# A chunk-attention and MLP kernel: half of tile 1's first product in seven products, its scores and side work moved

## The chip, the cores and the metric

The kernel runs on one core of a Trainium2 chip. The metric is the device time of one execution in microseconds. TensorE multiplies matrices into PSUM banks; VectorE, ScalarE and GpSimd (DVE, ACT and POOL in the profile) read and write them or on-chip memory; SyncE (SP) issues the DMAs. Each engine takes its instructions in order, and waits are made from the data dependencies of the program.

## The reference

Attention within chunks of 64 positions, then an MLP with exact Gelu:

```python
q_c = q.reshape(B, H, nc, 64, D)             # B = 8, H = 8, S = 576, D = 64, nc = 9
scores = scale * (q_c @ k_c.T);  attn = softmax(scores);  out = attn @ v_c
x = out.transpose(0, 2, 1, 3).reshape(B * S, H * D)      # 4608 x 512
y = gelu(x @ w_in) @ w_out                               # 512 -> 2048 -> 512
```

## The kernel before

The 4608 tokens are cut into nine tiles of 512: tile t below 8 has the first 512 positions of batch t, and tile 8 has the last chunk of each batch. Tiles are counted from 0. Work is in bf16 with float32 sums in PSUM. Each tile has two stages: `mm1` computes h = gelu(x w_in) as 16 slices of 128 hidden features, and `mm2` computes y = h w_out. The attention of tile t + 1 is put by hand between the matmuls of tile t; `phase(t, e1, e2)` gives what is put where, keyed by slot or by word.

**A plain slice** of `mm1` is four matmuls of 512 columns into one bank and a gelu on ScalarE (L470 for tiles 0 and 1, L595 in later ones).

**mm1 in groups** (L559, tiles 2 to 8) does half of the slices, in two groups a and b of four slices each, by Strassen's scheme in Winograd's form: seven products (`prod`, L572) of four matmuls of 256 columns each stand for the eight that four plain slices amount to. They use sums of blocks of w_in (made once, in tile 0) and of x (`x_sums`, L548: four subtractions on VectorE). The seven land in three banks X, Y, Z per group; between them copies and additions run. `PROGRAM` (L556) is the order, and its words are: `1a` is product 1 of group a; `c1a` copies X to a new Y on ScalarE; `c2a` copies Y out on ScalarE and `c3a` on VectorE (L616); `a1a` and `a2a` add Z to these copies on VectorE (L619); `g22a` is the gelu of a block (L590); `p` is a plain slice; `h1` to `h3` form sums of h, in tiles from 3 on. Product 3 accumulates in Y and waits until c3 has read it; product 4 accumulates in Z and waits until a1 has read it. The plain slices use the two banks of the pool `ps_tp`, products X and Z the three of `ps_at`, Y and the slots of mm2 the three of `ps_mm`.

**mm2** of tiles 1 and 2 has 16 slots of four matmuls of 512 columns; slot s computes quarter s % 4 of the sum for token block s // 4. From tile 3 on (`FIRST7`), mm2 too is done in seven products (L645), each of 16 matmuls of 256 columns, out of sums of w_out (`w_sums`) and of h.

**Attention of tile n** (called in mm2 of tile n - 1): `quad_S` (L223) computes the scores by 64 small matmuls into two banks of `ps_tp` and two of `ps_at`, and ScalarE takes four exps, after `act_table(Exp)` has loaded its table; `quad_parts` (L240) sums them by transposes and reductions on VectorE; `quad_total` goes on to the reciprocals; `quad_av` multiplies by v and `quad_x` writes the tile's x on VectorE. `x_sums` follows. In `one_tile` (L960), used for tiles 2 and 3, these stand at slots 0, 3 and 7 of mm2. From tile 3's mm2 on, `quad_av` stands behind the first of mm2's products and the scores of the tile after next behind the fourth.

**The k reorder.** k of tile 3 arrives transposed in another order of columns (`k_u`), and `in_order` (L195) copies it in four pieces on VectorE; the scores of tile 3 read the result.

Of the kernel before, what the change touches and what calls it, by code (L numbers as in the profile page):

```python
# [11 lines left out]
def kernel(  # L12
# [9 lines left out]
    nc = tc.nc  # L22
    P = 128
    f32 = mybir.dt.float32
    bf16 = mybir.dt.bfloat16
# [5 lines left out]
    J = 4  # L31
# [160 lines left out]
            st[nm + "t"] = flips.tile([P, G * J, P], bf16, tag=nm + "t", name=f"{nm}_t")  # L192
        nc.sync.dma_start_transpose(st[nm + "t"][:], st[nm][:].rearrange("p g j r d -> p (g j r d)"))  # L193

    def in_order(t):  # L195

        st = tiles[t]
        raw, st["kt"] = st["kt"], flips.tile([P, G * J, P], bf16, tag="kt", name="k_t")
        for g in range(G):
            DV(st["kt"][:, g * J:(g + 1) * J].rearrange("p n (e j) -> p (n e) j", j=J),  # L200
               raw[:, g * J:(g + 1) * J].rearrange("p j e -> p e j"))

# [264 lines left out]
        return T  # L467


    def mm1_slot(t, f, n=1, between={}):  # L470
        st = tiles[t]
        if f == 0:
            st["h"] = hpool.tile([P, FF, MT], bf16, tag="h", name="h")
        banks = [(ps_mm, "mm")] + [(ps_at, "at") if t == 1 else (ps_mm, "mm")] * (n - 1)
        h_ps = [pool.tile([P, MT], f32, tag=tag, name="h_ps") for pool, tag in banks]
        for ks in range(KS):
            for u in between.get(ks, ()):
                u()
            for a in range(n):
                o = f_of(t, f + a)  # L480
                nc.tensor.matmul(h_ps[a][:], w_in_sb[:, ks, o * P:(o + 1) * P], st["x"][:, ks, :],  # L481
                                 start=(ks == 0), stop=(ks == KS - 1))
        for a in range(n):
            nc.scalar.activation(st["h"][:, f_of(t, f + a), :], h_ps[a][:], Act.Gelu)  # L484

    def mm1_begin(t, n):

# [12 lines left out]
    def f_of(t, f):  # L500
        return f if t < FIRST7 else f // 2 + FH * (f % 2)

    def h_blocks(t, j0, j1):
        st = tiles[t]
# [40 lines left out]
        x = tiles[t]["x"][:].rearrange("p (c k) (n m) -> p c k n m", c=2, n=2)  # L545
        return x[:, 0, :, 0], x[:, 0, :, 1], x[:, 1, :, 0], x[:, 1, :, 1]

    def x_sums(t):  # L548

        b11, b12, b21, b22 = x_blocks(t)  # L550
        own = work.tile([P, 4, 2, TH], bf16, tag="x_t", name="x_t", bufs=1)
        T = tiles[t]["T"] = [None] + [own[:, i] for i in range(4)]
        for i, a, b in ((1, b12, b11), (3, b22, b12), (2, b22, T[1]), (4, b21, T[2])):
            nc.vector.tensor_tensor(T[i], a, b, op=mybir.AluOpType.subtract)
# [4 lines left out]
    def mm1_groups(t, extra):  # L559
# [5 lines left out]
        T, w = st["T"], in_blocks()  # L565
        TT, add = nc.vector.tensor_tensor, mybir.AluOpType.add
        banks, sums = {}, {}
        tags = {"a": ("y_1", "y_2"), "b": ("y_5", "y_2")}
        plain = [j + FH * r for j in (2, 3, 6, 7) for r in range(2)]
        hs = {"h1": (0, 4), "h2": (4, 7), "h3": (7, 8)}  # L570

        def prod(g, n):  # L572
            q = "ab".index(g)
            lhs, rhs, name, fresh = {
                1: (w[:, 0, :, 0, q], b11, "X", True), 2: (w[:, 1, :, 0, q], b21, "X", False),
                3: (w_s[4][:, :, q], b22, "Y", False), 4: (w[:, 1, :, 1, q], T[4], "Z", False),
                5: (w_s[1][:, :, q], T[1], "Y", False), 6: (w_s[2][:, :, q], T[2], "Y", False),
                7: (w_s[3][:, :, q], T[3], "Z", True)}[n]
            if fresh:
                banks[g + name] = ps_at.tile([P, 2, TH], f32, tag="at", name=f"h_{name}")  # L580
            for i in range(2):
                for kk in range(2):
                    nc.tensor.matmul(banks[g + name][:, i], lhs[:, kk, i], rhs[:, kk], start=fresh and i == kk == 0,  # L583
                                     stop=(kk == 1), skip_group_check=True)

        def gelu(g, r, m):
            j = 4 * "ab".index(g) + FH * r
            src = {(0, 0): lambda: banks[g + "X"], (0, 1): lambda: banks[g + "Y"],
                   (1, 0): lambda: sums[g, 0], (1, 1): lambda: sums[g, 1]}[r, m]()
            nc.scalar.activation(h[:, j:j + 2, m], src[:], Act.Gelu)  # L590

        for word in PROGRAM.split():
            for u in extra.get(word, ()):
                u()
            if word == "p":  # L595
                f = plain.pop(0)
                bank = ps_tp.tile([P, MT], f32, tag="tp", name="h_ps")
                for ks in range(KS):
                    nc.tensor.matmul(bank[:], w_in_sb[:, ks, f * P:(f + 1) * P], st["x"][:, ks, :],  # L599
                                     start=(ks == 0), stop=(ks == KS - 1))  # L600
                nc.scalar.activation(st["h"][:, f, :], bank[:], Act.Gelu)  # L601
            elif word in hs:
                if t >= FIRST7:
                    h_sums(t, *hs[word])
            elif word[0].isdigit():
                prod(word[1], int(word[0]))
            elif word[0] == "g":
                gelu(word[3], int(word[1]) - 1, int(word[2]) - 1)
            elif word[:2] == "c1":
                g = word[2]  # L610
                banks[g + "Y"] = ps_mm.tile([P, 2, TH], f32, tag="mm", name="h_Y")
                AC(banks[g + "Y"][:], banks[g + "X"][:])
            elif word[:2] in ("c2", "c3"):
                g, i = word[2], int(word[1]) - 2
                sums[g, i] = work.tile([P, 2, TH], f32, tag=tags[g][i], name=tags[g][i], bufs=1)
                (AC if i == 0 else DV)(sums[g, i][:], banks[g + "Y"][:])  # L616
            elif word[0] == "a":
                g, i = word[2], 2 - int(word[1])
                TT(sums[g, i][:], banks[g + "Z"][:], sums[g, i][:], op=add)  # L619
# [142 lines left out]
    def phase(t, extra1, extra2, by_rows=False, between={}, begun=0):  # L762
        nms = MT // P
        order = [(ms, qt) for ms in range(nms) for qt in range(NQ)]
        if by_rows:
            order = [(None, f) for f in range(FF - FC)] + [(ms, NQ - 1) for ms in range(nms)]
        first = begun or (3 if t == 1 else 1)
        if t >= FIRST71:
            mm1_groups(t, extra1)
        elif not begun:  # L770
            mm1_slot(t, 0, first, between)
        for f in range(first, FF if t < FIRST71 else 0):
            for u in extra1.get(f, ()):
                u()
            mm1_slot(t, f)
            if t >= FIRST7 and f in (7, 13, 15):
                h_sums(t, *{7: (0, 4), 13: (4, 7), 15: (7, 8)}[f])
# [61 lines left out]
    with tc.manual_schedule():  # L839
# [131 lines left out]

        pool_cast_qk(2)
        for t in range(1, NT):
# [4 lines left out]
            if t == 1:  # L978
# [3 lines left out]
                loads_of_qk(3)  # L982
                pool_cast_qk(3)
                load_v_rows(3)
                e1 = {3: [lambda: w_sums((1, 3))]}
                e2 = one_tile(2, {5: [lambda: act_table(Act.Gelu)],
                                  8: [lambda: flips_of(3), lambda: loads_of_qk(4)]})
            elif t == 2:
                cast_v_rows(3, PO)
                pool_cast_qk(4)  # L990
                e1 = {"3b": [lambda: in_order(3)], "h2": [lambda: w_sums((2, 4))]}
                flips_of(4)
                loads_at(2)
                cast_v_rows(4, PO)
# [2 lines left out]
            elif n < NT:  # L997
# [9 lines left out]
                else:  # L1007
# [44 lines left out]
```

## Time and profile before

| what | value |
|---|---|
| median of 3 runs | 278.72 us (278.70 to 278.88) |
| the profiled execution | 278.58 us |
| its span, first to last instruction | 276.8 us |
| mean granted TensorE clock | 0.997 |
| TensorE busy | 262.3 us, 95% |
| VectorE busy | 196.3 us, 71% |
| ScalarE busy | 172.9 us, 62% |

A line of the timeline has its start and length in microseconds, the engine, the source line, the operation, what it writes and reads, the tile's partitions and columns, and the count; in brackets stands the idle time of the engine before it and what ended it. Successive lines of TensorE overlap by its pipeline: the distance of two starts is what the stream costs, the length also holds the passage through the array.

### The profile page before, as it was taken

Reading aid. Unit: us, or ns where it says so; the run is one execution under the profiler, and the core shown is the slowest. Engines: PE = TensorE matmul, PEld = TensorE weight load, DVE = VectorE, ACT = ScalarE, POOL = GpSimd, SP = SyncE. Lnnn points to the kernel's source line nnn. Section 1 sums busy time; section 2 is a strip of 40 time slices with the busy share of each in tenths; the row PEclk is TensorE's granted clock in tenths of the full one; section 3 lists DMA queues with packets and bytes.
Section 4 is the critical chain, followed back from the end, with each engine's and each line's share of the span. In section 5 each row is a group of like instructions: output and inputs, shape, how many; then the busy total and the mean of one; then the engine's idle time right before and its main releaser. Section 6 shows DMA issues by size and latency. Waiting matters only on the chain.

```text
span 276.8 us, 7097 instructions
## 1 busy us (share of the span) xinstructions
PE 262.3 (95%) x2864; PEld 175.8 (64%) x2889; DVE 196.3 (71%) x348; ACT 172.9 (62%) x333; POOL 92.9 (34%) x180
## 2 busy tenths in 40 slices
PE   7789999999999699999999999999999999999993
PEld 3454454444456344668876887688768876886682
DVE  3664677901973999879967995899589958943842
ACT  2567746778638664886758666766675777328600
POOL 3635665541710823450372262108511311000000
PEclk9999999999999999999999999999999999999998
DMA  6999999998999977997999949896853310130005
GB/s 209 278 370 401 395 381 253 250 254 245 253 220 262 230 167 165 268 255 180 288 268 200 267 129 219 200 181 174 156 133 85 112 38 2 37 108 9 2 0 152
DMA packets 118064, 53.93 MB, mean 195 GB/s; under 512 B 93456, under 2 KB 112912, under 8 KB 118032
## 3 DMA queue, kind: packets, MB, share of 16 engines
q1 hardware_dynamic: 117712, 52.97, 73.0%
q8 instruction: 22, 0.36, 0.5%
q10 hardware_dynamic: 320, 0.52, 0.5%
q14 instruction: 10, 0.08, 0.1%
HBM read 36.70 MB, written 9.44 MB: 167 GB/s over the span
## 4 chain that ended last, share of the span: by engine, by line
PE 56%; DMA 14%; SPq 13%; DVE 7%; issue 3%; POOL 3%; ACT 2%; POOLq 0%; DVEq 0%; ACTq 0%
PE y_ps L637 23%; PE h_ps L599 14%; PE h_Y L583 6%; PE y_ps L735 5%; SPq L126 5%; DMA arrival<-in_q_dram 5%; DMA arrival<-in_v_dram 4%; PE h_X L583 4%; PE h_Z L583 4%; DMA arrival<-in_k_dram 3%; DMA arrival<-in_moe_w_in_dram 3%; SPq L193 2%; SPq L106 2%; SPq L112 2%; SPq L145 2%
## 5 line engine op out<-in xcount | busy, mean ns | idle before, releaser
L599 PE MATMUL h_ps<-x,w_in_sb 128*128 128x512 bf16 x211 | 54.7, 379 | 0.7
L601 ACT ACTIVATE h<-h_ps 128x512 bf16<-128x512 f32 x56 | 33.3, 595 | 14.8 <-PE h_ps L599 14.5
L637 PEld LDWEIGHTS <-h_s 128*128 128x128 bf16 x384 | 37.2, 98 | 4.6
L160 POOL CAST q_nat<-arrival 128x512 bf16<-128x512 f32 x33 | 22.2, 712 | 48.4 <-DMA arrival<-in_q_dram 33.3
L637 PE MATMUL y_ps<-w_t,h_s 128*128 128x256 bf16 x288 | 34.2, 273 | 0.2
L735 PE MATMUL y_ps<-w_out_sb,h 128*128 128x512 bf16 x138 | 31.3, 379 | 0.8 <-issue 0.8
L599 PEld LDWEIGHTS <-w_in_sb 128*128 128x128 bf16 x224 | 21.9, 98 | 16.0
L637 PEld LDWEIGHTS <-h 128*128 128x128 bf16 x288 | 28.2, 98 | 5.0 <-issue 0.5
L160 POOL CAST k_nat<-arrival 128x512 bf16<-128x512 f32 x34 | 23.3, 722 | 15.0 <-DMA arrival<-in_k_dram 9.3
L619 DVE TENSOR_TENSOR y<-h_Z,y 128x512 f32<-128x512 f32 x28 | 19.3, 690 | 10.9 <-PE h_Z L583 10.5
L583 PEld LDWEIGHTS <-w_in_s 128*128 128x128 bf16 x224 | 21.9, 98 | 8.0 <-issue 1.8
L481 PE MATMUL h_ps<-x,w_in_sb 128*128 128x512 bf16 x114 | 25.4, 379 | 0.5 <-DVE x L367 0.4
L207 POOL CAST v_nat<-arrival 128x1024 bf16<-128x1024 f32 x14 | 15.6, 1128 | 26.3 <-DMA arrival<-in_v_dram 26.3
L616 DVE COPY y<-h_Y 128x512 f32<-128x512 f32 x14 | 9.7, 691 | 19.9 <-PE h_Y L583 19.9
L735 PEld LDWEIGHTS <-h 128*128 128x128 bf16 x144 | 13.4, 98 | 15.6 <-issue 0.2
L637 PE MATMUL y_ps<-w_out_sb,h 128*128 128x256 bf16 x192 | 22.9, 273 | 0.0
L484 ACT ACTIVATE h<-h_ps 128x512 bf16<-128x512 f32 x29 | 17.0, 598 | 7.7 <-PE h_ps L481 7.6
L251 DVE STREAM_TRANSPOSE pt<-pT 128x256 f32<-128x256 f32 x28 | 12.2, 435 | 12.8 <-ACT pT L236 12.8
L837 ACT ACT_TABLE_LOAD x16 | 20.5, 1283 | 1.0 <-PEq L1036 0.7
L590 ACT ACTIVATE h<-y 128x512 bf16<-128x512 f32 x28 | 17.6, 627 | 5.7 <-DVE y L619 5.3
L583 PEld LDWEIGHTS <-w_in_sb 128*128 128x128 bf16 x168 | 16.4, 98 | 6.8
L481 PEld LDWEIGHTS <-w_in_sb 128*128 128x128 bf16 x116 | 11.3, 98 | 14.2 <-issue 0.7
(125 smaller groups left out, 446.4 us busy)
## 6 DMA issues: line engine op xcount, KB each, us to landing
out_dram<-y_sb SPq DMA_DIRECT2D x32, 256.0 KB, 2.9
arrival<-in_q_dram SPq DMA_DIRECT2D x7, 1024.0 KB, 6.3
arrival<-in_k_dram SPq DMA_DIRECT2D x24, 256.0 KB, 6.0
arrival<-in_v_dram SPq DMA_DIRECT2D x42, 128.0 KB, 3.1
arrival<-in_moe_w_out_dram SPq DMA_DIRECT2D x4, 1024.0 KB, 11.3
arrival<-in_v_dram SPq DMA_DIRECT2D x8, 256.0 KB, 5.8
arrival<-in_moe_w_in_dram SPq DMA_DIRECT2D x4, 512.0 KB, 7.6
arrival<-in_moe_w_in_dram SPq DMA_DIRECT2D x2, 1024.0 KB, 9.8
```

Source lines behind the costliest of these rows:

```text
L160: copy(st[nm][:, g].rearrange("p j r d -> p r j d"), st[nm + "f"][:, 2 * g:2 * g + 2])
L207: copy(st["v"][:, r::2], st["vf"][:, r::2])
L481: nc.tensor.matmul(h_ps[a][:], w_in_sb[:, ks, o * P:(o + 1) * P], st["x"][:, ks, :], start=(ks == 0), stop=(ks == KS - 1))
L484: nc.scalar.activation(st["h"][:, f_of(t, f + a), :], h_ps[a][:], Act.Gelu)
L583: nc.tensor.matmul(banks[g + name][:, i], lhs[:, kk, i], rhs[:, kk], start=fresh and i == kk == 0, stop=(kk == 1), skip_group_check=True)
L590: nc.scalar.activation(h[:, j:j + 2, m], src[:], Act.Gelu)
L599: nc.tensor.matmul(bank[:], w_in_sb[:, ks, f * P:(f + 1) * P], st["x"][:, ks, :], start=(ks == 0), stop=(ks == KS - 1))
L601: nc.scalar.activation(st["h"][:, f, :], bank[:], Act.Gelu)
L619: TT(sums[g, i][:], banks[g + "Z"][:], sums[g, i][:], op=add)
L637: nc.tensor.matmul(out[m], lhs[:, f, m * P:(m + 1) * P], rhs[:, f, :], start=fresh and f == 0 and (m == 0 or len(out) == 3), stop=(f == FH ...
L735: nc.tensor.matmul(y_ps[:], st["h"][:, f, ms * P:(ms + 1) * P], w_out_sb[:, f, :], start=(f == 0), stop=(f == FF - 1))
L837: nc.scalar.activation(act_scratch[:], rest[:, 0:1], func)
```

## The change

- Tile 1's mm1 is done in groups too (`FIRST71` 1 instead of 2), by an order of its own, `LATE`. It begins with three plain slices worked together (`start`, as tile 1 did before) and then forms the sums of x of tile 1 (`sums`). It has no `p` between 7b and 2b or between 3b and 4b, and no `p` after 4b. The banks of `p` are those of `ps_tp`.
- `w_sums((1, 3))` moves from behind tile 1's first three slices to the end of its mm1.
- `quad_S` and `quad_parts` of tiles 2 and 3 move from slot 0 to slot 1 of mm2; `act_table(Exp)` stays at slot 0.
- The four copies of `in_order(3)`, all at the word `3b` of tile 2, are done two at `3b` and two at `g21b`, so that `a2b` stands between them.
- In mm2 of tiles 3 to 7, `x_sums` is done as (1, 3) and (2, 4), with the addition at L678 and its store between the two.

```diff
-    def in_order(t):
+    def in_order(t, g0):
         st = tiles[t]
-        raw, st["kt"] = st["kt"], flips.tile([P, G * J, P], bf16, tag="kt", name="k_t")
-        for g in range(G):
+        if g0 == 0:
+            st["k_u"], st["kt"] = st["kt"], flips.tile([P, G * J, P], bf16, tag="kt", name="k_t")
+        raw = st["k_u"]
+        for g in (g0, g0 + 1):
...
-    FIRST7, FIRST71 = 3, 2
+    FIRST7, FIRST71 = 3, 1
...
-    def x_sums(t):
+    def x_sums(t, which=(1, 3, 2, 4)):
...
+        of = {1: (b12, b11), 3: (b22, b12), 2: (b22, T[1]), 4: (b21, T[2])}
+        for i in which:
+            a, b = of[i]
             nc.vector.tensor_tensor(T[i], a, b, op=mybir.AluOpType.subtract)

     PROGRAM = """begin 1a c1a 7a p 2a 6a c2a g11a 1b c1b p 5a c3a a1a 7b p 2b g22a 6b c2b 3a g11b g12a 4a a2a
                  p g21a 5b c3b a1b totals rc0 p 3b g22b g12b p 4b h1 a2b p g21b h2 p h3"""
+    LATE = """begin start sums p 1a c1a 7a p 2a 6a c2a g11a 1b c1b p 5a c3a a1a 7b 2b g22a 6b c2b 3a g11b g12a 4a a2a
+              p g21a 5b c3b a1b p 3b g22b g12b 4b a2b g21b end"""
...
-        for word in PROGRAM.split():
+        for word in (LATE if t == 1 else PROGRAM).split():
             for u in extra.get(word, ()):
                 u()
+            if word == "start":
+                mm1_slot(t, [plain.pop(0) for _ in range(3)], between)
+            elif word == "sums":
+                x_sums(t)
...
-            at = {0: [lambda: act_table(Act.Exp), lambda: quad_S(n), lambda: quad_parts(n)],
+            at = {0: [lambda: act_table(Act.Exp)], 1: [lambda: quad_S(n), lambda: quad_parts(n)],
...
-                e1 = {3: [lambda: w_sums((1, 3))]}
+                e1 = {"end": [lambda: w_sums((1, 3))]}
...
-                e1 = {"3b": [lambda: in_order(3)], "h2": [lambda: w_sums((2, 4))]}
+                e1 = {"3b": [lambda: in_order(3, 0)], "g21b": [lambda: in_order(3, 2)], "h2": [lambda: w_sums((2, 4))]}
...
-                      2: [lambda: x_sums(n)]}
+                      2: [lambda: x_sums(n, (1, 3))], 3: [lambda: x_sums(n, (2, 4))]}
...
-                    e2[3] = [lambda: quad_part(n + 1, 0, 0), lambda: quad_part(n + 1, 0, 1)]
+                    e2[3] += [lambda: quad_part(n + 1, 0, 0), lambda: quad_part(n + 1, 0, 1)]
```

More of the change, by code (lines that the diff above doesn't have):

```diff
@@ L467, in att_units, with mm1_slot @@
         return T
-    def mm1_slot(t, f, n=1, between={}):
+    def mm1_slot(t, fs, between={}):
         st = tiles[t]
-        if f == 0:
+        if "h" not in st:
             st["h"] = hpool.tile([P, FF, MT], bf16, tag="h", name="h")
-        banks = [(ps_mm, "mm")] + [(ps_at, "at") if t == 1 else (ps_mm, "mm")] * (n - 1)
+        banks = [(ps_mm, "mm")] + [(ps_at, "at")] * (len(fs) - 1)
         h_ps = [pool.tile([P, MT], f32, tag=tag, name="h_ps") for pool, tag in banks]
@@ L478, in mm1_slot @@
                 u()
-            for a in range(n):
-                o = f_of(t, f + a)
-                nc.tensor.matmul(h_ps[a][:], w_in_sb[:, ks, o * P:(o + 1) * P], st["x"][:, ks, :],
+            for a, f in enumerate(fs):
+                nc.tensor.matmul(h_ps[a][:], w_in_sb[:, ks, f * P:(f + 1) * P], st["x"][:, ks, :],
                                  start=(ks == 0), stop=(ks == KS - 1))
-        for a in range(n):
-            nc.scalar.activation(st["h"][:, f_of(t, f + a), :], h_ps[a][:], Act.Gelu)
+        for a, f in enumerate(fs):
+            nc.scalar.activation(st["h"][:, f, :], h_ps[a][:], Act.Gelu)
     def mm1_begin(t, n):
@@ L546, in x_blocks @@
         return x[:, 0, :, 0], x[:, 0, :, 1], x[:, 1, :, 0], x[:, 1, :, 1]
-    def x_sums(t):
+    def x_sums(t, which=(1, 3, 2, 4)):
         b11, b12, b21, b22 = x_blocks(t)
-        own = work.tile([P, 4, 2, TH], bf16, tag="x_t", name="x_t", bufs=1)
-        T = tiles[t]["T"] = [None] + [own[:, i] for i in range(4)]
-        for i, a, b in ((1, b12, b11), (3, b22, b12), (2, b22, T[1]), (4, b21, T[2])):
+        if "T" not in tiles[t]:
+            own = work.tile([P, 4, 2, TH], bf16, tag="x_t", name="x_t", bufs=1)
+            tiles[t]["T"] = [None] + [own[:, i] for i in range(4)]
+        T = tiles[t]["T"]
+        of = {1: (b12, b11), 3: (b22, b12), 2: (b22, T[1]), 4: (b21, T[2])}
+        for i in which:
+            a, b = of[i]
             nc.vector.tensor_tensor(T[i], a, b, op=mybir.AluOpType.subtract)
@@ L557, with mm1_groups @@
                  p g21a 5b c3b a1b totals rc0 p 3b g22b g12b p 4b h1 a2b p g21b h2 p h3"""
-    def mm1_groups(t, extra):
+    LATE = """begin start sums p 1a c1a 7a p 2a 6a c2a g11a 1b c1b p 5a c3a a1a 7b 2b g22a 6b c2b 3a g11b g12a 4a a2a
+              p g21a 5b c3b a1b p 3b g22b g12b 4b a2b g21b end"""
+    def mm1_groups(t, extra, between={}):
         st = tiles[t]
@@ L564, in mm1_groups @@
         b11, b12, b21, b22 = x_blocks(t)
-        T, w = st["T"], in_blocks()
+        w = in_blocks()
         TT, add = nc.vector.tensor_tensor, mybir.AluOpType.add
@@ L573, in prod @@
             q = "ab".index(g)
[L574 to L578, printed above, removed]
+            if n in (1, 2):
+                lhs, rhs, name = w[:, n - 1, :, 0, q], b11 if n == 1 else b21, "X"
+            elif n == 3:
+                lhs, rhs, name = w_s[4][:, :, q], b22, "Y"
+            elif n == 4:
+                lhs, rhs, name = w[:, 1, :, 1, q], st["T"][4], "Z"
+            else:
+                lhs, rhs, name = w_s[n - 4][:, :, q], st["T"][n - 4], "Z" if n == 7 else "Y"
+            fresh = n in (1, 7)
             if fresh:
@@ L590, in gelu @@
             nc.scalar.activation(h[:, j:j + 2, m], src[:], Act.Gelu)
-        for word in PROGRAM.split():
+        for word in (LATE if t == 1 else PROGRAM).split():
             for u in extra.get(word, ()):
                 u()
-            if word == "p":
+            if word == "start":
+                mm1_slot(t, [plain.pop(0) for _ in range(3)], between)
+            elif word == "sums":
+                x_sums(t)
+            elif word == "p":
                 f = plain.pop(0)
@@ L766, in phase @@
             order = [(None, f) for f in range(FF - FC)] + [(ms, NQ - 1) for ms in range(nms)]
-        first = begun or (3 if t == 1 else 1)
         if t >= FIRST71:
[L769 to L777, printed above, removed]
+            mm1_groups(t, extra1, between)
+        else:
+            for f in range(begun, FF):
+                mm1_slot(t, [f])
         if t >= FIRST7:
```

2 lines of the change are left out of this document (removed).

## The prediction

> **What bounds the kernel now.** Tiles are counted from 0. I read the page first, then the engines' busy time by stage, then TensorE's list of waits, and last the merged timeline around each place that the diff touches.
>
> ```profile
> PE 262.3 (95%) x2864; PEld 175.8 (64%) x2889; DVE 196.3 (71%) x348; ACT 172.9 (62%) x333; POOL 92.9 (34%) x180
> ```
> ```profile
> 50.67:65.10 14.43, 14.01 (x64) 6.16 (x63) 4.64 (x7) 10.17 (x18) 5.47 (x8) 1.00 1.00 233
> 65.10:80.37 15.27, 15.06 (x192) 7.45 (x193) 11.94 (x24) 9.72 (x24) 7.66 (x11) 1.00 0.89 262
> 80.37:93.61 13.24, 13.13 (x87) 8.49 (x87) 7.28 (x11) 9.75 (x18) 3.17 (x4) 1.00 1.04 238
> 93.61:111.86 18.25, 15.72 (x254) 8.04 (x257) 16.79 (x28) 10.69 (x27) 6.84 (x7) 1.00 0.81 188
> ```
> ```profile
> PE s_ps L229 <- ACT h L601: 2.1, 1, 2.1
> PE y_ps L637 <- DVE y_sb L678: 0.3, 1, 0.3
> ```
>
> The second fence has mm1 of tile 1, mm2 of tile 1, mm1 of tile 2 and mm2 of tile 2, with length and busy time of PE, PEld, DVE, ACT and POOL. TensorE fills three of the four; mm2 of tile 2 is 18.25 us long with 15.72 busy. The third fence gives the reason: one wait of 2.1 us before tile 3's scores. So the time is the sum of what TensorE streams plus a few waits, and in mm2 of tile 2 VectorE (16.79 of 18.25) is nearly as full as TensorE. That last fact limits the gain below.
>
> **Part 1: mm1 of tile 1 in groups.**
>
> ```profile
> 52.50 12.68 PE L481 MATMUL h_ps<-x,w_in_sb 128*128 128x512 bf16 x57 [0.37 <-DVE x L367]
> 52.96 2.34 DVE L631 TENSOR_TENSOR w_t<-w_out_sb 128x2048 bf16<-128x2048 bf16 x2
> 65.21 0.60 ACT L484 ACTIVATE h<-h_ps 128x512 bf16<-128x512 f32 x1 [0.27 <-PE h_ps L481]
> 67.23 2.04 ACT L236 ACTIVATE pT<-s_ps 128x512 bf16<-128x512 f32 x4
> 67.84 0.45 DVE L251 STREAM_TRANSPOSE pt<-pT 128x256 f32<-128x256 f32 x1 [12.54 <-ACT pT L236]
> 78.68 1.24 DVE L554 TENSOR_TENSOR x_t<-x 128x512 bf16<-128x512 bf16 x2
> 80.81 0.60 PE L583 MATMUL h_Z<-x_t,w_in_s 128*128 128x256 bf16 x4
> 82.11 0.60 PE L583 MATMUL h_X<-x,w_in_sb 128*128 128x256 bf16 x4
> 82.54 0.60 PE L583 MATMUL h_Y<-x_t,w_in_s 128*128 128x256 bf16 x4
> ```
>
> One record of the 58 matmuls from 52.50 to 65.10 is missing: 12.60/58 is close to 0.216 us for a matmul of 512 columns, 0.864 for a plain slice of four. A product of four matmuls of 256 columns takes 82.54 - 82.11 = 0.43 to 0.44 (0.109 each). The change removes 8 plain slices (6.91 us) and adds 14 products (6.11): TensorE saves 0.80.
>
> By the sustained spacing in the Trainium skill's page "TensorE: Matmul & The Clock Gate", section "Back-to-back issue gap" (131 ns at 512 columns, 81 at 128, so an estimate of 98 at 256 on a straight line), 32 matmuls of 4.2 us would become 56 of 5.5 us, 1.3 us lost instead of 0.8 won. The trace disagrees with both figures here: 216 and 109 ns.
>
> Waits come back. The first twelve matmuls are as before and end at 52.50 + 6 x 0.216 = 53.80. The new sums of x (two at 1.24 together, two shorter) start on VectorE where w_sums stood, at 52.96, so the one that the second product needs is there at 54.2; a plain slice and the first product lie ahead of it, to 55.1. They cost nothing, by 0.9 us of cover. At the end, tile 2's rows show what the new order does:
>
> ```profile
> 89.06 1.03 PE L599 MATMUL h_ps<-x,w_in_sb 128*128 128x512 bf16 x4
> 89.32 0.69 DVE L616 COPY y<-h_Y 128x512 f32<-128x512 f32 x1 [0.66 <-PE h_Y L583]
> 90.04 0.69 DVE L619 TENSOR_TENSOR y<-h_Z,y 128x512 f32<-128x512 f32 x1
> 90.06 0.60 PE L583 MATMUL h_Y<-x,w_in_s 128*128 128x256 bf16 x4
> ```
>
> There the plain slice ends at 89.93 and product 3b starts at 90.06, when c3b has read its bank: 0.13 lost. LATE has the same slice there, but none between 3b and 4b. 3b would end at 90.50 and 4b cannot write before a1b has read the bank, at 90.73: 0.25 to 0.30 lost. With 0.05 for small hand-offs earlier, the rest of mm1 takes 5 x 0.864 + 14 x 0.436 + 0.13 + 0.28 + 0.05 = 10.9 and ends at 64.7 instead of 65.10: 0.40 won, half of the 0.80.
>
> ScalarE ends later. It has 20 operations from 53.6 on (8 plain gelus, 8 of products, 4 copies); at 0.60 each that is 65.6. The last gelu waits for a2b: 4b ends at 64.7, VectorE starts 0.25 later (as c3b in the rows above), 0.69, then a gelu of 0.63: 66.3. Now the last gelu ends at 65.81 and the exps start 1.42 later, behind the table load. So the exps of tile 2 move from 67.23 to 67.7, 0.5 later. Putting the scores one slot later costs nothing: they are then done by 66.5 (64.7, 0.86 for the slot, twice 0.45 for such scores in part 2's rows), ahead of the table. w_sums (1, 3), moved behind a2b, runs from 65.6 to 68.0 on a VectorE that waits for the first exp until 68.3 (67.84 and 0.5): hidden, by 0.3 us. From the exps VectorE works without a gap to the sums of x, so the one that tile 2's second product needs slips from 79.92 to 80.4, while TensorE would want it at 80.81 - 0.40 = 80.4. The slack of 0.9 is used up exactly. I take 0.05 of wait: **0.35 won** at tile 2's second product.
>
> **Part 2: end of tile 2's mm1, scores of tile 3.**
>
> ```profile
> 90.65 3.67 DVE L200 COPY k_t<-k_u 128x512 bf16<-128x512 bf16 x4
> 91.36 0.60 PE L583 MATMUL h_Z<-x_t,w_in_sb 128*128 128x256 bf16 x4
> 93.61 0.45 PE L229 MATMUL s_ps<-q_t,k_t 64*64 64x64 bf16 x32
> 94.24 0.68 DVE L619 TENSOR_TENSOR y<-h_Z,y 128x512 f32<-128x512 f32 x1
> 94.84 2.96 DVE L631 TENSOR_TENSOR w_t<-w_out_sb,w_t 128x2048 bf16<-128x2048 bf16 x2
> 94.95 0.63 ACT L590 ACTIVATE h<-y 128x512 bf16<-128x512 f32 x1 [1.50 <-DVE y L619]
> 95.49 0.58 ACT L601 ACTIVATE h<-h_ps 128x512 bf16<-128x512 f32 x1
> 96.12 0.45 PE L229 MATMUL s_ps<-q_t,k_t 64*64 64x64 bf16 x32 [2.06 <-ACT h L601]
> 96.72 5.99 PE L735 MATMUL y_ps<-w_out_sb,h 128*128 128x512 bf16 x27 [0.16 <-issue]
> 98.10 0.45 DVE L251 STREAM_TRANSPOSE pt<-pT 128x256 f32<-128x256 f32 x1 [0.30 <-ACT pT L236]
> ```
>
> The 2.06 us is a queue of three. The scores' second half needs the bank of the last plain slice; its gelu stands on ScalarE behind g21b; g21b needs a2b; a2b stands on VectorE behind all four copies of the k reorder, 3.67 us, though its product 4b was done near 92. After: two copies end at 92.1 (everything 0.35 earlier), a2b at 92.8, g21b at 93.5, the last gelu, ready when mm1 ends at 93.26, near 94.1. TensorE meanwhile runs slot 0 of mm2, to 94.1. What is late next is the other half of k: copies from 92.8 to 94.6. The scores' first half starts at 94.1, the second at about 94.65, and slot 1 starts at 95.2. Before, slot 1 started at 96.72 + 0.86 = 97.58. TensorE is 2.4 us ahead, 0.35 of it from part 1.
>
> **VectorE takes some back.** It did 3.67 + 0.68 + 2.96 in a row and does the same work in another order. Of 2.4 us it gains 0.35 and the idle 0.30 ahead of the transposes: they start at 97.5 instead of 98.10.
>
> ```profile
> 108.94 1.59 DVE L554 TENSOR_TENSOR x_t<-x 128x512 bf16<-128x512 bf16 x2
> 112.07 0.69 DVE L746 COPY y_sb<-y_ps 128x512 f32<-128x512 f32 x1 [0.74 <-PE y_ps L735]
> 112.30 0.60 PE L583 MATMUL h_Z<-x_t,w_in_s 128*128 128x256 bf16 x4
> 117.68 0.69 DVE L619 TENSOR_TENSOR y<-h_Z,y 128x512 f32<-128x512 f32 x1
> 118.82 0.60 PE L583 MATMUL h_Z<-x_t,w_in_sb 128*128 128x256 bf16 x4
> ```
>
> The sum of x for tile 3's second product was ready at 110.53, will be at 109.9, and is wanted at 112.30 - 2.4 = 109.9: nearly no wait. VectorE goes on without a gap to a1a of tile 3; the only idle time left there, 0.74 for the row copy at 112.07, goes as well. a1a ends at 118.37 - 0.6 - 0.74 = 117.03. Product 4a, which it releases, stood at 118.82 with 0.45 to spare and now starts at 117.08: **1.74 won, not 2.4**. Afterwards both engines wait for each other in turns as before, and this difference stays.
>
> **Part 3: sums of x in two.**
>
> ```profile
> 187.90 1.59 DVE L554 TENSOR_TENSOR x_t<-x 128x512 bf16<-128x512 bf16 x2
> 189.45 1.91 PE L637 MATMUL y_ps<-w_out_sb,h_s 128*128 128x256 bf16 x16
> 190.91 0.68 DVE L678 TENSOR_TENSOR y_sb<-y_ps,y 128x512 f32<-128x512 f32 x1
> 191.65 1.91 PE L637 MATMUL y_ps<-w_t,h 128*128 128x256 bf16 x16 [0.28 <-DVE y_sb L678]
> ```
>
> In tiles 3 to 7 the addition at L678 stood behind all four sums. Only in tile 5 did TensorE wait: its 16 matmuls (1.75 us) end their stream at 191.20, the next start at 191.65. With two sums behind the addition it ends over a microsecond earlier: **0.45 won**. The two moved sums are needed only in the next tile, over a microsecond after that; the transposes behind them start when they did. Nothing is priced for them.
>
> **Sum.** 0.35 + (1.74 - 0.35) + 0.45 = 2.2 us. The profiled execution took 278.58 (span 276.8), so 276.4; the median of the runs shown is 0.14 higher: **276.5**.
>
> **Rivals.** *VectorE does not take it back.* If tile 3's a1a comes with TensorE (transposes and reductions that are slowed less by GpSimd's casts elsewhere), all of 2.4 + 0.45 stays: 275.9. Against it: VectorE's row of 16.79 busy in 18.25. Chance 0.13.
>
> *ScalarE sets mm1 of tile 1.* My ScalarE times let operations follow each other closely. If each takes its full 0.60 and waits behind the one ahead, the last gelu ends 0.65 later than I have it, the copies release the banks 0.2 later, and tile 1 loses 0.25 instead of winning 0.35: 277.1. For it: 20 operations in 12 us. Chance 0.20.
>
> *The wait only moves.* The deferral is not enough, because the last gelu still comes late or k is late, and the loss of the rival above comes too. VectorE's chain then gains its idle 1.04 at most and tile 1 gives most of it back: 278.4, no difference. Chance 0.07.
>
> *Slower: VectorE late for tile 2's second product.* The place is w_sums (1, 3) in front of tile 2's transposes. Every microsecond by which the first transpose starts after 68.3 is waited for at tile 2's second product. The change ends above the old time by more than 0.56 if that start is later than 71.0 (2.2 of gain to eat, 0.56 beyond). At the slower rate of w_sums (2, 4), 2.96, the start is 68.6; with ScalarE 0.65 late it is 69. So this needs two unseen microseconds; at 71.2 the time is 279.4. Weight loads of 24 more matmuls, if they showed, are of this kind too; tile 2's 13.24 us in 32 plain matmuls (6.91) and 56 small ones (6.11), 13.02 in all, leave them no room. Chance 0.08.
>
> **How the numbers follow.** Forecast 0.52, rivals 0.13, 0.20, 0.07, 0.08. 0.2% is 0.56 us, about what a measurement here can tell. Faster: 0.52 + 0.13 + 0.20 = 0.85; same 0.07; slower 0.08. The range runs from 275.6, the first rival with 0.3 to spare, to 277.6, the second with 0.5 for tile 5's wait that might stay.
>
> **What would show it.** In the changed profile: mm1 of tile 1 is about 14.0 us long, with waits at 3b and 4b for VectorE (L616, L619). The wait of s_ps for L601 is gone, and scores of tile 3 wait at most some tenths for the k copies. VectorE has no idle time from tile 2's c3b to tile 3's a1a, and 4a (or 3a) of tile 3 waits for it. L678 no longer appears among TensorE's waits. The forecast is wrong if tile 1's mm1 is longer than 14.4, if tile 2's second product waits over 0.5 us for a sum of x, or if tile 3's mm1 starts less than a microsecond earlier.

## Result, and the profile after

The changed kernel takes 276.26 us, median of 20 runs (275.5 to 280.27), beside 278.86 (20 runs, 276.63 to 282.53) for the kernel before: ratio 0.9915, 95% interval 0.9892 to 0.9938. The forecast was 276.5.

The profiled execution that came with this result was among the longest of its kernel, 279.33 us with a span of 277.4. From its page, the granted clock of TensorE in 40 slices, in tenths of full speed:

```profile
PEclk9559999999999999999999999999999999999999
```

The two fives lie between 7 and 21 us, ahead of everything that was changed; the last section comes back to them. So the changed kernel was profiled again, twice, as a1_changed (276.41 us) and a2_changed (275.82). The stages of a1_changed, with the columns of the windows of before (mm1 of tile 1, mm1 of tile 2, mm2 of tile 2):

```profile
50.77:64.75 13.98, 13.40 (x89) 8.52 (x88) 7.36 (x14) 10.71 (x21) 5.56 (x9) 1.00 1.00 239
80.11:93.55 13.44, 13.33 (x90) 8.52 (x89) 8.26 (x14) 10.03 (x20) 2.83 (x5) 1.00 1.05 245
93.55:109.77 16.22, 16.22 (x257) 7.96 (x256) 15.63 (x27) 10.50 (x27) 6.72 (x7) 1.00 0.83 193
```

mm1 of tile 1 went from 14.43 to 13.98. mm2 of tile 2 went from 18.25 to 16.22, and TensorE now fills it. `mm1` of tile 2 became 0.20 longer, and VectorE has 0.59 us left in mm2 of tile 2.

What happens before 50 us differs between executions, so the traces are compared from one point in tile 1 on: the start of the second half of its first twelve matmuls (52.50 in the profile before, 52.60 in a1_changed, 52.24 to 56.12 in all traces), which no edit here reaches. From TensorE's timeline, in us from that point. The columns "tile 2" and "tile 3" have the first product of the tile, "end" has the end of the last matmul, and a length runs from a tile's first product to that of the next:

```
                  tile 2   tile 3   end      length of tile 2   3      4      5
before            27.87    59.36    219.72   31.49            27.03  27.03  27.47
changed, after    27.51    56.79    216.70   29.28            27.03  27.02  27.04
a1_changed        27.51    57.17    217.16   29.66            27.03  27.03  27.10
a2_changed        27.50    57.08    217.07   29.58            27.12  27.02  27.03
e1_plain1         27.88    57.16    217.08   29.28            27.03  27.03  27.03
e2_k_once         27.51    58.36    218.31   30.85            27.02  27.03  27.03
e3_slot0          27.50    57.39    217.29   29.89            27.03  27.02  27.03
e4_x_once         27.51    56.80    217.07   29.29            27.02  27.32  27.10
e5_quiet          27.82    59.68    225.40   31.86            28.16  31.70  27.03
e6_t3first        27.50    56.79    216.70   29.29            27.03  27.03  27.02
e7_best           27.09    56.62    215.80   29.53            26.91  26.90  26.93
e8_best_again     27.18    56.97    216.79   29.79            27.51  26.90  26.97
```

So the 2.6 to 3.0 us of gain are 0.36 in tile 1, 1.8 to 2.2 in tile 2 and 0.4 in tile 5.

### The profile page after: what moved, and what is told of

Read it like the earlier page. It is cut to its first block, busy times and chain, and to the rows that moved or that the text cites. A ratio compares the mean times of both kernels' runs of the same rounds, so it can differ in the third digit from the quotient of the medians.

```text
span 277.4 us, 7189 instructions
## 1 busy us (share of the span) xinstructions
PE 267.3 (96%) x2913; PEld 180.8 (65%) x2913; DVE 199.1 (72%) x358; ACT 174.0 (63%) x337; POOL 90.3 (33%) x180
## 4 chain that ended last, share of the span: by engine, by line
PE 90%; DVE 3%; DMA 2%; ACT 2%; issue 1%; SPq 0%; POOL 0%; ACTq 0%; DVEq 0%
PE y_ps L650 27%; PE h_ps L612 19%; PE y_ps L748 10%; PE h_Y L592 8%; PE h_Z L592 5%; PE h_X L592 5%; PE h_ps L482 5%; PE y_ps L772 4%; DMA arrival<-in_k_dram 2%; PE s_ps L231 2%; PE tp L166 2%; PE rc_ps L429 1%; ACT y_ps L678 1%; PE h_ps L494 1%; DVE x L369 1%; DVE rc L408 1%
## 5 line engine op out<-in xcount | busy, mean ns | idle before, releaser
L612 PE MATMUL h_ps<-x,w_in_sb 128*128 128x512 bf16 x244 | 61.5, 379 | 0.0
L614 ACT ACTIVATE h<-h_ps 128x512 bf16<-128x512 f32 x61 | 36.4, 597 | 15.3 <-PE h_ps L612 15.0
L612 PEld LDWEIGHTS <-w_in_sb 128*128 128x128 bf16 x244 | 23.9, 98 | 17.5
L632 DVE TENSOR_TENSOR y<-h_Z,y 128x512 f32<-128x512 f32 x32 | 22.1, 690 | 12.4 <-PE h_Z L592 11.9
L592 PEld LDWEIGHTS <-w_in_s 128*128 128x128 bf16 x256 | 25.0, 98 | 9.1 <-issue 2.0
L629 DVE COPY y<-h_Y 128x512 f32<-128x512 f32 x16 | 11.0, 691 | 21.4 <-PE h_Y L592 21.4
L592 PEld LDWEIGHTS <-w_in_sb 128*128 128x128 bf16 x192 | 18.8, 98 | 7.8 <-issue 0.3
L599 ACT ACTIVATE h<-y 128x512 bf16<-128x512 f32 x32 | 20.1, 628 | 5.6 <-DVE y L632 5.2
L256 DVE TENSOR_REDUCE part<-pt 128x16 f32<-128x512 bf16 x28 | 19.2, 686 | 1.0
L592 PE MATMUL h_Y<-x_t,w_in_s 128*128 128x256 bf16 x128 | 19.2, 273 | 0.0
L592 PE MATMUL h_X<-x,w_in_sb 128*128 128x256 bf16 x128 | 19.2, 273 | 0.0
L308 DVE TENSOR_TENSOR x<-av_ps,rc 128x512 bf16<-128x512 f32 x28 | 18.0, 669 | 0.6
```

What stands on the lines that cost most here:

```text
L256: nc.vector.tensor_reduce(st["part", g2][:, c, :, :, 0], pt[:].rearrange("p n e u -> p n u e"), axis=mybir.AxisListType.X, op=mybir.AluOpT ...
L308: nc.vector.tensor_tensor(x.rearrange("p n (e u) -> p n e u", u=2), st["av"][g2][c][:].rearrange("p n (e u) -> p n e u", u=2), st["rc", 2 ...
```

## Experiments

Each edit is against the changed kernel. Times are medians, ratios are to the kernel before with their 95% interval.

**The changed kernel itself, twice.**

> The changed kernel itself once more, for a trace beside the others. In the profiled execution shown so far TensorE was 3.6 us late before tile 1 began, and its clock was granted at half speed in the first 22 us. Theory V (VectorE does not cap the gain): counted from the second half of tile 1's first twelve matmuls, tile 3's first product starts 2.4 to 2.7 us earlier than in the kernel before. Theory C (VectorE caps it, as forecast): tile 3's product 4a waits for VectorE and starts 1.7 us earlier. Time 276.3 by both, within 0.6.

> The changed kernel beside the reordered one, on the same chip. From the second half of tile 1's first twelve matmuls to the end 216.7 to 217.2 us, as in its two traces so far; time 276.0 to 276.3.

a1_changed 276.03 us (0.9898, 0.9854 to 0.9943), a2_changed 276.14 (0.9901, 0.9866 to 0.9937). In a1_changed tile 3's first product and its product 4a are both 2.19 us earlier than before, between what the two theories asked for; in the first profile both are 2.57 earlier, which is Theory V. The places that the forecast named, in a1_changed's merged timeline. First the end of mm1 of tile 1:

```profile
62.84 0.69 DVE L629 COPY y<-h_Y 128x512 f32<-128x512 f32 x1 [0.66 <-PE h_Y L592]
63.57 0.69 DVE L632 TENSOR_TENSOR y<-h_Z,y 128x512 f32<-128x512 f32 x1
63.59 0.60 PE L592 MATMUL h_Y<-x,w_in_s 128*128 128x256 bf16 x4
64.32 0.60 PE L592 MATMUL h_Z<-x_t,w_in_sb 128*128 128x256 bf16 x4
64.75 1.03 PE L748 MATMUL y_ps<-w_out_sb,h 128*128 128x512 bf16 x4
65.56 2.35 DVE L644 TENSOR_TENSOR w_t<-w_out_sb 128x2048 bf16<-128x2048 bf16 x2
65.68 0.63 ACT L599 ACTIVATE h<-y 128x512 bf16<-128x512 f32 x1 [0.26 <-DVE y L632]
67.73 1.55 ACT L238 ACTIVATE pT<-s_ps 128x512 bf16<-128x512 f32 x3
68.34 0.45 DVE L253 STREAM_TRANSPOSE pt<-pT 128x256 f32<-128x256 f32 x1 [0.43 <-ACT pT L238]
```

Product 3b starts when c3b has read its bank, 4b (64.32) when a1b has: 63.57 + 0.69 = 64.26. From 3b to 4b pass 0.73 us where the stream takes 0.44. All of this is the forecast's chain. Next, tile 2's second product, in a1_changed, and after it the same sums in the first profile of the changed kernel:

```profile
79.11 1.04 POOL L209 CAST v_nat<-arrival 128x1024 bf16<-128x1024 f32 x1 [1.76 <-DMA arrival<-in_v_dram]
79.18 1.58 DVE L556 TENSOR_TENSOR x_t<-x 128x512 bf16<-128x512 bf16 x2
80.11 0.60 PE L592 MATMUL h_X<-x,w_in_sb 128*128 128x256 bf16 x4
80.82 0.61 PE L592 MATMUL h_Z<-x_t,w_in_s 128*128 128x256 bf16 x4
```
```profile
82.71 0.75 DVE L556 TENSOR_TENSOR x_t<-x 128x512 bf16<-128x512 bf16 x2
```

The second product starts 0.71 after the first instead of 0.44: 0.27 of wait for the sums, which end at 80.76. The same two sums take 1.58 us here and 0.75 there. In a1_changed GpSimd casts v beside them, in the other profile it does not, and there the product follows in 0.43. Last, the end of tile 2's mm1:

```profile
90.68 1.52 DVE L202 COPY k_t<-k_u 128x512 bf16<-128x512 bf16 x2
92.13 0.68 DVE L632 TENSOR_TENSOR y<-h_Z,y 128x512 f32<-128x512 f32 x1
92.73 1.91 DVE L202 COPY k_t<-k_u 128x512 bf16<-128x512 bf16 x2
93.90 0.59 ACT L614 ACTIVATE h<-h_ps 128x512 bf16<-128x512 f32 x1
94.50 0.83 PE L231 MATMUL s_ps<-q_t,k_t 64*64 64x64 bf16 x64
94.56 2.77 DVE L644 TENSOR_TENSOR w_t<-w_out_sb,w_t 128x2048 bf16<-128x2048 bf16 x2
95.27 5.35 PE L748 MATMUL y_ps<-w_out_sb,h 128*128 128x512 bf16 x24
97.24 0.43 DVE L253 STREAM_TRANSPOSE pt<-pT 128x256 f32<-128x256 f32 x1
```

a2b (92.13) stands between the halves of k; the last gelu starts at 93.90 instead of 95.49, and the scores run in one piece. They are a tenth late because the second half of k ends at 94.64.

**e1_plain1: tile 1 without groups**, the rest of the change kept.

```diff
-    FIRST7, FIRST71 = 3, 1
+    FIRST7, FIRST71 = 3, 2
...
-            for f in range(begun, FF):
+            if not begun:
+                mm1_slot(t, [0, 1, 2], between)
+            for f in range(begun or 3, FF):
...
+            for u in extra1.get("end", ()):
+                u()
```

> Only mm1 of tile 1 goes back to 16 plain slices; everything else as changed. If tile 1 wins the 0.35 us that the forecast gave it, the time is 0.35 above the changed kernel; if the waits at 3b and 4b are hidden by something, 0.8 above; if ScalarE sets tile 1's groups (rival), 0.25 below.

276.41 us, ratio 0.9898 (0.9849 to 0.9947), beside 276.03 and the same ratio of the changed kernel on the same chip: the runs do not tell the two apart. From the common point, tile 2's first product comes at 27.88: the groups' 0.36 is gone. But its second product waits for nothing, tile 2 is 29.28 long instead of 29.66, and the end is at 217.08, as in a1_changed and a2_changed (217.16, 217.07). So in these executions the groups' gain is lost again to the late sum of x and the late k; where the sums are quick (216.70) it stays. The groups' net worth is between nothing and 0.4 us.

**e2_k_once: all four copies of k together again.**

```diff
-                e1 = {"3b": [lambda: in_order(3, 0)], "g21b": [lambda: in_order(3, 2)], "h2": [lambda: w_sums((2, 4))]}
+                e1 = {"3b": [lambda: in_order(3, 0), lambda: in_order(3, 2)], "h2": [lambda: w_sums((2, 4))]}
```

> Only the k reorder goes back to four copies at 3b, ahead of a2b; the scores stay at slot 1. By the queue of three (a2b behind the copies, the gelu behind a2b), the scores' second half waits again, about 2.06 less the 0.9 of slot 0: 0.9 to 1.3 us above the changed kernel on TensorE. Theory C: VectorE's work is the same in any order, so tile 3 gives 0.6 of it back and the time is 0.4 to 0.7 above. If the copies' order is of no matter, no difference.

277.53 us, ratio 0.996 (0.9927 to 0.9994). Its timeline at the end of tile 2's mm1:

```profile
90.99 3.83 DVE L202 COPY k_t<-k_u 128x512 bf16<-128x512 bf16 x4
94.75 0.68 DVE L632 TENSOR_TENSOR y<-h_Z,y 128x512 f32<-128x512 f32 x1
95.46 0.63 ACT L599 ACTIVATE h<-y 128x512 bf16<-128x512 f32 x1 [1.66 <-DVE y L632]
96.62 0.45 PE L231 MATMUL s_ps<-q_t,k_t 64*64 64x64 bf16 x32 [1.36 <-ACT h L614]
```

The queue of three is back: copies, a2b, g21b, last gelu, scores. Tile 2 is 30.85 long, 1.2 to 1.3 more than in a1_changed and a2_changed. More than half of part 2's gain is the split of k. The end is 1.15 and 1.24 later than in those two traces, as the queue of three had it (0.9 to 1.3), and not the 0.4 to 0.7 of Theory C.

**e3_slot0: scores of tiles 2 and 3 back in slot 0.**

```diff
-            at = {0: [lambda: act_table(Act.Exp)], 1: [lambda: quad_S(n), lambda: quad_parts(n)],
+            at = {0: [lambda: act_table(Act.Exp), lambda: quad_S(n), lambda: quad_parts(n)],
```

> Only the scores of tiles 2 and 3 go back to slot 0; the k copies stay split. In tile 2 the scores' second half then waits for the last plain slice's gelu, ready about 0.9 us after mm1's end: TensorE loses 0.7 to 1.0. Theory V: the time is 0.7 to 1.0 above the changed kernel. Theory C: VectorE would have taken 0.65 of it anyway, 0.1 to 0.4 above. For tile 1 nothing, since the scores' banks are free by then.

276.25 us, ratio 0.9902 (0.9867 to 0.9937). In its timeline the wait is small:

```profile
93.75 0.59 ACT L614 ACTIVATE h<-h_ps 128x512 bf16<-128x512 f32 x1
94.39 0.44 PE L231 MATMUL s_ps<-q_t,k_t 64*64 64x64 bf16 x32 [0.45 <-ACT h L614]
```

Tile 2 is 0.23 to 0.31 longer than in a1_changed and a2_changed, 0.6 longer than where nothing delays it (29.28). I had expected 0.7 to 1.0 on TensorE. The last gelu ends at 94.34, 0.84 behind the start of the scores at 93.50, about as expected; but the scores' first half fills part of that, and the slot hides less than I priced. Tile 3's first product and its 4a are both 1.97 earlier than before, so VectorE took nothing back: Theory C's 0.1 to 0.4 has the number without its reason. The medians do not tell e3_slot0 from the changed kernel.

**e4_x_once: all four sums of x ahead of the addition.**

```diff
-                      2: [lambda: x_sums(n, (1, 3))], 3: [lambda: x_sums(n, (2, 4))]}
+                      2: [lambda: x_sums(n)], 3: []}
```

> Only the sums of x in mm2 of tiles 3 to 7 go back to four at once. If the addition behind them was what TensorE waited for in tile 5, that tile's length (first product to the next tile's first product) is 27.4 to 27.5 us instead of 27.0 to 27.1, and the time is 0.4 above the changed kernel. Rival: the wait came from GpSimd's casts slowing VectorE in that stretch of that one execution, and depends on where they fall: then tile 5 is 27.0 to 27.2 and there is no difference.

276.88 us, ratio 0.993 (0.9891 to 0.9969). The wait came back, but in tile 4 and not in tile 5. Its timeline in tile 4:

```profile
156.81 3.66 POOL L160 CAST q_nat<-arrival 128x512 bf16<-128x512 f32 x4 [8.59 <-issue]
158.42 1.57 DVE L556 TENSOR_TENSOR x_t<-x 128x512 bf16<-128x512 bf16 x2
159.91 1.29 DVE L556 TENSOR_TENSOR x_t<-x,x_t 128x512 bf16<-128x512 bf16 x2
161.12 0.68 DVE L691 TENSOR_TENSOR y_sb<-y_ps,y 128x512 f32<-128x512 f32 x1
159.82 1.91 PE L650 MATMUL y_ps<-w_out_sb,h_s 128*128 128x256 bf16 x16
161.85 1.91 PE L650 MATMUL y_ps<-w_t,h 128*128 128x256 bf16 x16
```

The matmuls' stream ends at 159.82 + 1.75 = 161.57 and the next start at 161.85, after the addition. GpSimd's casts fall on the sums, which take 1.57 and 1.29, and the addition is late. Which tile waits depends on where the casts fall, as the rival had it. The medians do not tell e4_x_once from the changed kernel: the intervals overlap.

**e5_quiet: GpSimd held back** until w_sums (2, 4) of tile 2 are done, by a cast of one element of their result ahead of its work there.

```diff
+    pool_scratch = consts.tile([P, 1], f32, name="pool_scratch")
...
-                pool_cast_qk(4)
+                def held():
+                    PO(pool_scratch[:], w_t[4][:, 0, 0:1])
+                    pool_cast_qk(4)
+                    flips_of(4)
+                    loads_at(2)
+                    cast_v_rows(4, PO)
-                e1 = {"3b": [lambda: in_order(3, 0)], "g21b": [lambda: in_order(3, 2)], "h2": [lambda: w_sums((2, 4))]}
-                flips_of(4)
-                loads_at(2)
-                cast_v_rows(4, PO)
+                e1 = {"3b": [lambda: in_order(3, 0)], "g21b": [lambda: in_order(3, 2)],
+                      "h2": [lambda: w_sums((2, 4)), held]}
```

> GpSimd's casts of q and k of tile 4 are held back until VectorE has done the second pair of w_out sums in tile 2; nothing else differs from the changed kernel. Theory: these casts slow VectorE's operations in on-chip memory. Then the four k copies take about 2.2 us (0.55 each) instead of 3.4, the w_out sums about 2.4 instead of 2.8 to 2.9, and the scores of tile 3 wait for no copy. VectorE is then over a microsecond earlier at tile 3, which TensorE uses only as far as it waited there: time 0 to 0.2 below the changed kernel. Rival: the copies are slow by their own strides; they keep 3.4 and 2.8.

284.12 us, ratio 1.0187 (1.0155 to 1.0219): as a version it fails, far from the 0 to 0.2 below the changed kernel that were forecast. Tiles 2, 3 and 4 are 31.86, 28.16 and 31.70 long; I put it down to the loads that were held with the casts. Its durations still answer the question. VectorE's timeline there:

```profile
94.77 1.11 DVE L202 COPY k_t<-k_u 128x512 bf16<-128x512 bf16 x2
96.72 1.11 DVE L202 COPY k_t<-k_u 128x512 bf16<-128x512 bf16 x2
97.75 2.48 DVE L644 TENSOR_TENSOR w_t<-w_out_sb,w_t 128x2048 bf16<-128x2048 bf16 x2
```

With GpSimd idle, two copies of k take 1.11 us (1.52 and 1.91 in a1_changed) and w_sums 2.48 (2.77). TensorE's largest wait of this run is this:

```profile
PE av_ps L301 <- ACT h L614: 3.8, 2, 2.9
```

The casts of v that it needs stand behind the held work on GpSimd, so I read it as a wait for them and not for the ScalarE operation named; that was not tried by itself.

**e6_t3first: the sum for product 7 first**, in the hope of removing the wait of 0.27.

```diff
-    def x_sums(t, which=(1, 3, 2, 4)):
+    def x_sums(t, which=(3, 1, 2, 4)):
...
-                      2: [lambda: x_sums(n, (1, 3))], 3: [lambda: x_sums(n, (2, 4))]}
+                      2: [lambda: x_sums(n, (3, 1))], 3: [lambda: x_sums(n, (2, 4))]}
```

> The changed kernel with the sums of x in the order 3, 1, 2, 4, so that the one that the second product needs is made first. If the wait of tile 2's second product (0.27 in the last trace) is for that sum, it goes, and the time is 0.2 to 0.3 below the changed kernel; if it is for the sum of the bank's release or another, it stays.

276.62 us, ratio 0.9897 (0.9868 to 0.9926). No wait, and an end at 216.70; but in this trace the two sums took 0.76 together, since no cast met them, and with 0.75 the old order does not wait either. It settles nothing about the order.

**e7_best and e8_best_again (one kernel, twice): the waits at 3b and 4b filled**, on top of e6's order. In both word lists c2b goes ahead of g22a, and a slice moves between a1b and 3b.

```diff
-                 p g21a 5b c3b a1b totals rc0 p 3b ...
+                 5b c3b a1b p g21a totals rc0 p 3b ...
...
-              p g21a 5b c3b a1b p 3b g22b g12b 4b a2b g21b end"""
+              5b c3b a1b p g21a p 3b g22b g12b 4b a2b g21b end"""
```

> As the last, and the orders of mm1 in groups changed: c2b ahead of g22a, product 5b directly behind 4a, so that two plain slices instead of one lie between 5b and 3b (in tile 1 and in all others). If the waits at 3b (0.13 in each tile) and at 4b in tile 1 (0.29) are for VectorE's c3b and a1b alone, they go: 0.4 in tile 1 and 0.13 in each of seven tiles, 1.2 to 1.3 us below the last kernel. Rival: ScalarE then releases 5b's bank too late (c2b), and the wait moves to 5b, no gain.

> The reordered groups once more, beside the changed kernel. If the order removes the waits at 3b and 4b whatever the start of the execution does, 215.8 us from the same point to the end, 0.9 to 1.3 less than the changed kernel in the same job. Rival: the difference of the last traces was where GpSimd's casts fell; then the two agree within 0.3.

275.82 us, ratio 0.9871 (0.9832 to 0.9909), and 275.88, ratio 0.9895 (0.9859 to 0.9932). The end of mm1 of tile 1 in e7_best:

```profile
64.66 0.60 PE L592 MATMUL h_Y<-x,w_in_s 128*128 128x256 bf16 x4
65.10 0.60 PE L592 MATMUL h_Z<-x_t,w_in_sb 128*128 128x256 bf16 x4
65.53 1.03 PE L748 MATMUL y_ps<-w_out_sb,h 128*128 128x512 bf16 x4
```

3b and 4b now follow at 0.44, tile 1 is 0.33 to 0.42 shorter than in the changed kernel, and from tile 3 on a tile that nothing delays takes 26.90 instead of 27.03. Tile 2 is longer (29.53 and 29.79 beside 29.28). The end is at 215.80 in e7_best, but at 216.79 in e8_best_again, whose tile 3 is 27.51 long. Among its waits:

```profile
PE h_X L592 <- ACT h_Y L625: 0.5, 1, 0.5
PE h_Y L592 <- DVE y L629: 0.2, 1, 0.2
```

The first is product 2a of tile 2, which waits for c1a on ScalarE; that part of the order was not changed. The second is product 3a of tile 3, which waits for c3a on VectorE. The median of e7_best is 0.80 below e6_t3first on the same chip, where 1.2 to 1.3 were forecast, and that of e8_best_again 0.26 below a2_changed, which is the rival's "within 0.3". The intervals overlap each time: not shown to be faster.

## Why the prediction was right, step by step

**Tile 1's groups: 0.40 forecast, 0.36 measured** at tile 2's first product. The two waits at the end were worked out as 0.13 and 0.28 and are there. The last gelu ends at 66.31 (forecast 66.3), the exps start at 67.73 (67.7), the first transpose at 68.34 (68.3), w_sums end at 67.91 (68.0); a1_changed runs 0.10 later as a whole. What did not come out is the label: TensorE's list does not put 3b's and 4b's waits under VectorE's lines. A matmul of 256 columns is 0.27 long in the profile at a distance of 0.11, so a delay of 0.13 leaves no idle time in the record, and one of 0.29 only 0.13. That the waits are real shows in e7_best, where they go.

**Tile 2's second product: 0.05 of wait forecast, 0.27 in a1_changed and 0.28 in a2_changed, at most 0.04 in every other trace.** The sums start when the forecast has them (79.18; before 78.68, and 0.5 later). The step that was mis-sized is their duration: I carried over 1.24 us from the profile before, and it is 0.75 to 1.59 depending on GpSimd. The 1.24 was such a case itself: the first of the two took 0.91, beside a cast of v. The rival "VectorE late for tile 2's second product" has this mechanism and this place, at about a tenth of its price (0.27 of the 2.9 us that lay between it and the forecast); w_sums in front of the transposes, the cause it gave, cost nothing.

**Scores and the halves of k: the wait of 2.06 is gone**, in the order forecast. Slot 1 starts at 95.27, 95.17 on the old clock, forecast 95.2. e2_k_once shows that the split of k is the larger half of part 2; what the later slot adds (e3_slot0) shows in the traces alone, 0.2 to 0.6 us, and not in the medians.

**"VectorE takes some back": the step that failed.** The forecast had TensorE 2.4 us ahead and VectorE let only 1.74 of it through at product 4a of tile 3. Both numbers are off. TensorE's own lead in a1_changed was 2.20: slot 0 before starts at 96.51, right after the scores, and not at 96.72; the row's "0.16 <-issue" with 27 of 28 matmuls is a missing first record. And VectorE's chain was shorter than I had it. The rows of a1a and product 4a in a1_changed, then in the first profile of the changed kernel:

```profile
115.99 0.69 DVE L632 TENSOR_TENSOR y<-h_Z,y 128x512 f32<-128x512 f32 x1
116.73 0.60 PE L592 MATMUL h_Z<-x_t,w_in_sb 128*128 128x256 bf16 x4
```
```profile
118.73 0.69 DVE L632 TENSOR_TENSOR y<-h_Z,y 128x512 f32<-128x512 f32 x1
119.87 0.60 PE L592 MATMUL h_Z<-x_t,w_in_sb 128*128 128x256 bf16 x4
```

a1a in a1_changed ends at 116.68, 116.58 on the old clock, where I had 117.03. The idle 0.30 and 0.74 went as forecast. The rest is the k copies and w_sums: from the first copy to the end of w_sums 6.65 us (90.68 to 97.33) instead of 7.15 (90.65 to 97.80). I had them do "the same work in another order" for the same price; e5_quiet shows that this price is set by GpSimd's casts, and that another 1.2 us of it would go without them (94.77 to 100.23 there, 5.46).

So the cap of 1.74 acts in none of the three traces of this kernel. In a1_changed and a2_changed VectorE's a1a and TensorE's 4a meet within 0.1 us, 2.19 earlier than before: a1_changed's 4a has waited for nothing, a2_changed's for 0.1, so VectorE is about to be the limit there. In the first profile a1a ends 0.45 ahead of 4a, as it did before the change, VectorE idles 0.89 for TensorE at the row copy, and 4a is 2.57 earlier: no cap at all. What separates 2.57 from 2.19 lies further ahead, the late sum of x (0.27) and the late k (0.1). The operations that the rival "VectorE does not take it back" named are not what varies: transposes (0.43) and reductions (0.69) take the same beside casts as without them.

**The addition at L691: 0.45 forecast, 0.37 to 0.44 measured** in tile 5's length, and it is gone from TensorE's waits. The row in a1_changed:

```profile
187.69 0.69 DVE L691 TENSOR_TENSOR y_sb<-y_ps,y 128x512 f32<-128x512 f32 x1 [0.70 <-ACT pT L238]
189.18 1.91 PE L650 MATMUL y_ps<-w_t,h 128*128 128x256 bf16 x16
```

It ends 0.8 us ahead of the matmuls that need it. e4_x_once adds that the wait can fall in another tile (0.3 in tile 4), not in tile 5 as such.

**The sum** was 2.2 us by 0.35, 1.39 and 0.45; from the common point a1_changed wins 2.56 by 0.36, 1.83 and 0.37, the first profile 3.02 by 0.36, 2.21 and 0.43, and the medians 2.60. The likeliest case and the rival "VectorE does not take it back" (275.9) lie on either side of the median. The traces have that rival's course, without the cap. That the time is still within 0.3 us of 276.5 is in part luck: the second term was too small by 0.44 to 0.82, and the late sum, which the forecast had at 0.05, took 0.27 of TensorE's lead in two of the three traces.

## What to carry to other kernels

When a wait is a queue of several engines, find the link that stands behind work it does not need and move that work, as the two k copies behind a2b: this took more than half of the wait away and one more slot the rest. Before saying that an engine "takes it back", compare the new finish times of both engines link by link, take an operation's duration as a span of values if another engine's work runs beside some of its samples, and count a row's records before reading its start. A gain of a few tenths ahead of an engine without slack is kept in one execution and lost in the next.

## What was not expected of the hardware

**VectorE's copies and sums within on-chip memory and GpSimd's casts wait for each other.** Two sums of x: 0.75 or 1.58 us. Two k copies: 1.11 with GpSimd idle, 1.52 to 1.91 beside it. The copy at L629 and the addition at L632, which read TensorE's banks, take 0.68 or 0.69 in every trace, also where a cast runs beside them, as beside the addition at 92.13. That GpSimd is the cause is shown by e5_quiet for the k copies and w_sums; for the sums of x it rests on which traces have a cast at that moment. It goes both ways: four casts of q take 2.29 us in e5_quiet after VectorE's w_sums, and 3.42 in a1_changed beside the k copies.

```profile
90.77 3.42 POOL L160 CAST q_nat<-arrival 128x512 bf16<-128x512 f32 x4 [10.61 <-DMA arrival<-in_q_dram]
```
```profile
100.41 2.29 POOL L160 CAST q_nat<-arrival 128x512 bf16<-128x512 f32 x4
```

Taken one at a time, the operations of a1_changed take turns. The first sum of x, the second k copy and the second cast of q:

```profile
79.18 1.25 DVE L556 TENSOR_TENSOR x_t<-x 128x512 bf16<-128x512 bf16 x1
91.19 1.01 DVE L202 COPY k_t<-k_u 128x512 bf16<-128x512 bf16 x1
91.70 0.98 POOL L160 CAST q_nat<-arrival 128x512 bf16<-128x512 f32 x1
```

The sum starts 0.07 behind the cast of v (79.11 to 80.15) and ends 0.28 behind its end; the next sum, with no cast beside it, takes 0.41. The cast of v takes its usual 1.04, the mean of all fourteen in this profile. The k copy starts within the first cast of q (90.77 to 91.75) and ends 0.45 behind it; the second cast of q starts within this copy and ends 0.48 behind it. So the later operation waits for the earlier one to end. A rate shared evenly by the two would have made the cast of v longer too.

The Trainium skill's page "SBUF — State Buffer", section "Who interferes with whom", has a rule for this: VectorE and GpSimd share a pair of ports as an exclusive lock, for copies in a two-port mode and for operations with two inputs in on-chip memory against a GpSimd operation that reads it, and the later one waits for the earlier to end; with at most one such input and outside that mode, VectorE does not contend. The rows agree: the sum that meets a cast of 1.04 us waits for its end, 0.83 lost, and L629 and L632 lose nothing. Whether the k copies run in a two-port mode is not shown by a run here.

**A granted clock lowered near the start costs more than the change wins.** In the first profile of the changed kernel, the second q is cast at 6.91 us (6.29 in a1_changed) and TensorE idles 1.31 for it. The granted clock of that execution is then 0.5 for two slices, a1_changed's is not lowered, and tile 1's common point comes at 56.12 instead of 52.60: 3.5 us, more than the whole change wins. From that point on, that execution is as quick as any of the changed kernel (216.70). The idle time does not decide it by itself: in e8_best_again TensorE idles 1.07 at the same place, and its clock is not lowered. The row in the first profile, then in e8_best_again:

```profile
7.40 0.40 PE L166 MATMUL tp<-ident,q_nat 128*128 128x128 bf16 x4 [1.31 <-DVE q_nat L160]
```
```profile
7.18 0.40 PE L166 MATMUL tp<-ident,q_nat 128*128 128x128 bf16 x4 [1.07 <-DVE q_nat L160]
```

The other way round, e6_t3first idles 0.64 there, as a1_changed does (0.66), and its clock is lowered in the second slice (0.7). What lowers it stays open.
